# Reordering the attention steps, the range of the logits and the first gather of a fused HGRN2 and expert-routing kernel

## The chip, the cores and the metric

The kernel runs on one core of a Trainium2 chip, as one launch. The metric is the device time in microseconds (us). Before the change the median of three runs is 498.82 us (498.05 to 499.04); the profiled execution took 495.89 us, of which the trace spans 494.1 us. TensorE is called PE in profiles, its weight loads PEld; VectorE is DVE, ScalarE ACT, GpSimd POOL, SyncE SP.

## The reference

A gated linear attention (HGRN2) with 4 batches, 8 heads, 768 positions and a head size of 48 is followed by a layer of 8 experts with balanced assignment.

```python
def _attn_ref(q, k, v, f_logit):
    f = 1.0 / (1.0 + np.exp(-f_logit))
    state = np.zeros((B, H, D, D)); y = np.zeros_like(q)
    for t in range(S):
        state = f[:, :, t, :, None] * state + np.einsum('bhd,bhe->bhde', k[:, :, t], v[:, :, t])
        y[:, :, t] = np.einsum('bhd,bhde->bhe', q[:, :, t], state)
    return y

def _moe_ref(x, w_gate, w1, w2):          # x: 3072 tokens of 384
    logits = x @ w_gate                    # 3072 x 8
    # greedy: the largest logits first; each token gets one expert,
    # each expert takes at most cap = 3072 / 8 = 384 tokens
    for idx in np.argsort(-logits.flatten()): ...
    for e in range(E):
        out[assigned == e] = np.maximum(x[assigned == e] @ w1[e], 0.0) @ w2[e]
```

## The kernel before

The attention works on 24 chunks of 128 positions (6 for each of 4 batches). Each chunk runs through stages; a step holds one stage each of up to six chunks. The order of the parts is written down by hand, and each engine takes its instructions in this order. The number behind each part is its stage: how many steps ago its chunk began.

```python
    STEP = ((decayed, 2), (q_columns, 2), (k_columns, 2), (sums, 1), (transposed, 5),
            (factors, 1), (x_copy, 5), (k_copy, 2),
            (added, 2), (halves, 1), (gate, 5), (gated_q, 1), (new_state, 2), (decays, 0),
            (gated_k, 1), (span, 1), (to_logits, 5), (split, 0), (clamp, -1), (outputs, 4),
            (scores, 3))
    small = deque()

    def attention(first, last):
        for step in range(first, last):
            if step + AHEAD < len(chunks):
                load(chunks[step + AHEAD])
            for part, stage in STEP:
                if 0 <= step - stage < len(chunks):
                    part(chunks[step - stage])
                if part is split:
                    for _ in range(min(len(small), 4)):
                        small.popleft()()
```

`small` is a queue of little operations, constants for the routing at first, that are slipped into the steps. What the parts put on the engines:

- `q_columns`, `k_columns`: transposes T on TensorE; ScalarE copies qT, and `k_copy` on VectorE copies kT.
- `sums`: the products L of the decays with a triangle. `factors`: VectorE cuts them off (dl), ScalarE takes the exponentials eq and ek.
- `transposed`, `x_copy`, `gate`, `to_logits`: the finished rows x are transposed to X, VectorE copies xT, TensorE multiplies by the gate weights, VectorE copies the logits.
- `added`, `new_state`: the products dS of k and v for the carried state. `halves`: sums of the decays over half chunks, into the same bank as X. `span` copies these.
- `decays` (ScalarE), `split`: upper on VectorE, then high on ScalarE and low on GpSimd, the two terms for the next `sums`.
- `scores`: the products A of k and q, 32 small matmuls, and two masked copies am on VectorE.
- `outputs`: the values (am with v) and the state products (R with qT) in Y, and two copies of x on ScalarE:

```python
    def outputs(G):
        b, c = G["b"], G["c"]
        x = work.tile([128, D], FP32, name="x", tag="x", bufs=3)
        Y = [ps("Y", "sum") for _ in range(2)]
        for hp in range(HP):
            ...                      # Y <- am, v
        if G["R"] is not None:       # not in the first chunk of a batch
            ...                      # Y <- R, qT
        for par in range(2):
            nc.scalar.copy(out=..., in_=Y[par]...)
        row = S * b + C * c
        nc.scalar.dma_start(out=xd[row:row + C, :], in_=x[:])
        G["x"] = x
```

Near the end of the attention the range of the logits is found (`bounds`), for the thresholds of the search that follows. It takes two little matmuls:

```python
        def extremes():
            r = ps("bounds")
            ts(pair[:, 1:2], pair[:, 1:2], -1.0, ALU.mult)
            nc.tensor.transpose(out=r[0:2, 0:128], in_=pair[:], identity=ident[:])
            reduce(top[0:2, :], r[0:2, 0:128], ALU.max)
            ts(tops[0:2, :], ident[0:2, 0:2], top[0:2, :], ALU.mult)

        def spread():
            r = ps("bounds")
            nc.tensor.matmul(out=r[:, 0:2], lhsT=two[0:2, :], rhs=tops[0:2, :], start=True,
                             stop=True)
            nc.vector.tensor_copy(out=ends[:], in_=r[:, 0:2])
            reduce(width[:], ends[:], ALU.add)
        ...
        return [partial(lanes, 0, ALU.max), partial(lanes, 1, ALU.min), extremes, spread,
                one_step] + [partial(table, shift) for shift in SHIFTS]
```

Then come 8 rounds of routing, each with a search in five counting steps (`digit_alone` in the first round, `digit_beside` with expert matmuls between them later) and a list of the tokens of one expert: members, places, lines, comparisons in_line with the counts, and the token numbers. With these the rows xe are gathered from DRAM by an indirect DMA that GpSimd issues. `idle_turns(n, ...)` puts n matmuls of constants on TensorE; their result is not used.

```python
            def place():
                incl = rt([NT], "mincl")
                nc.vector.tensor_tensor_scan(incl[:], onesc[:], L["member"][:], 0.0,
                                             op0=ALU.mult, op1=ALU.add)
                total = rt([1], "total", BF16)
                nc.vector.tensor_copy(out=total[:], in_=incl[:, NT - 1:NT])
                r = bank("before", "r")
                nc.tensor.matmul(out=r[:, 0:1], lhsT=ltri[:], rhs=total[:], start=True, stop=True)
            ...
            def lines():
                stt(pl[:], L["incl"][:], L["r"][:, 0:1], L["member"][:], ALU.add, ALU.mult)
                tt(b[:], col(pl[:], TE - 1), row(beyond_block[:], TE - 1), ALU.is_ge)
                for i in range(TE - 2):
                    stt(pl[:], b[:, :, i], -128.0, pl[:], ALU.mult, ALU.add)
                stt(line[:], b[:, :, TE - 2], -128.0, pl[:], ALU.mult, ALU.add)
```

Of the kernel before, what the change touches and what calls it, by code (L numbers as in the profile page):

```python
# [11 lines left out]
FP32 = mybir.dt.float32  # L12
# [14 lines left out]
def kernel(  # L27
# [289 lines left out]
    def outputs(G):  # L317
        b, c = G["b"], G["c"]
        x = work.tile([128, D], FP32, name="x", tag="x", bufs=3)
        Y = [ps("Y", "sum") for _ in range(2)]  # L320
        for hp in range(HP):
            for par in range(2):
                for j in range(2):
# [4 lines left out]
                        start=(hp == 0), stop=False, skip_group_check=True)  # L328
        if G["R"] is not None:
# [9 lines left out]
        for par in range(2):  # L339
            nc.scalar.copy(  # L340
                out=x[:].rearrange("t (a r d) -> t r a d", r=2, d=DH)[:, par],
                in_=Y[par][:, 0:HP * DH].rearrange("t (a d) -> t a d", d=DH))
        row = S * b + C * c
        nc.scalar.dma_start(out=xd[row:row + C, :], in_=x[:])
        G["x"] = x
# [20 lines left out]
    def to_logits(G, to=None):  # L366
        if to is None:
# [11 lines left out]
    STEP = ((decayed, 2), (q_columns, 2), (k_columns, 2), (sums, 1), (transposed, 5),  # L379
            (factors, 1), (x_copy, 5), (k_copy, 2),  # L380
            (added, 2), (halves, 1), (gate, 5), (gated_q, 1), (new_state, 2), (decays, 0),
            (gated_k, 1), (span, 1), (to_logits, 5), (split, 0), (clamp, -1), (outputs, 4),
            (scores, 3))
    small = deque()

    def attention(first, last):
        for step in range(first, last):
            if step + AHEAD < len(chunks):
                load(chunks[step + AHEAD])
            for part, stage in STEP:  # L390
                if 0 <= step - stage < len(chunks):
                    part(chunks[step - stage])
                if part is split:
                    for _ in range(min(len(small), 4)):
                        small.popleft()()
# [38 lines left out]
    def ramp(n, name, step, base, when=later):  # L434
# [8 lines left out]
    later(nc.vector.tensor_copy, out=counts[:],  # L443
          in_=count_i[:].unsqueeze(2).to_broadcast((128, 128, 2)))
# [16 lines left out]
    beyond_block = ramp(TE - 1, "beyond_block", 128, 1)  # L461
# [66 lines left out]
    def bounds(c1):  # L528
# [6 lines left out]

        def lanes(at, op):
# [3 lines left out]

        def extremes():
            r = ps("bounds")
            ts(pair[:, 1:2], pair[:, 1:2], -1.0, ALU.mult)
            nc.tensor.transpose(out=r[0:2, 0:128], in_=pair[:], identity=ident[:])
            reduce(top[0:2, :], r[0:2, 0:128], ALU.max)
            ts(tops[0:2, :], ident[0:2, 0:2], top[0:2, :], ALU.mult)

        def spread():
            r = ps("bounds")
            nc.tensor.matmul(out=r[:, 0:2], lhsT=two[0:2, :], rhs=tops[0:2, :], start=True,  # L550
                             stop=True)
            nc.vector.tensor_copy(out=ends[:], in_=r[:, 0:2])
# [642 lines left out]
```

## Time and profile before

| stage | us from the start | what sets the pace |
|---|---|---|
| filling and regular steps | 0 to 119 | TensorE, with short waits |
| steps with the range of the logits | 119 to 152 | TensorE and VectorE in turn |
| drain of the attention | 152 to 173 | a chain through VectorE and TensorE |
| first routing and gather | 173 to 200 | VectorE, then the gather |
| experts and 7 more rounds | 200 to 494 | TensorE |

The page of the profile has these totals:

```text
PE 449.5 (91%) x4873; PEld 305.7 (62%) x4873; DVE 267.3 (54%) x890; ACT 137.6 (28%) x323; POOL 139.2 (28%) x195
DMA  8999998765001104417117027036045046701000
GB/s 169 194 207 208 200 203 191 171 148 127 35 19 41 44 2 165 140 28 274 50 57 262 34 82 255 16 122 213 17 140 195 17 149 215 294 11 38 0 27 27
```

Each digit or number is one fortieth of the span, 12.35 us. In lines of the timeline the columns are the start in us, the time until the last instruction of the group ends, the engine, the line of the kernel, the operation, output and inputs with their shapes, and the count. What stands in brackets is the idle time before the group, and which instruction ended it. Busy time of matmuls overlaps, as they are pipelined, so starts are better compared than durations.

### The profile page before, as it was taken

Reading aid. Unit: us, or ns where it says so; the run is one execution under the profiler, and the core shown is the slowest. Engines: PE = TensorE matmul, PEld = TensorE weight load, DVE = VectorE, ACT = ScalarE, POOL = GpSimd, SP = SyncE. Lnnn points to the kernel's source line nnn. Section 1 sums busy time; section 2 is a strip of 40 time slices with the busy share of each in tenths; the row PEclk is TensorE's granted clock in tenths of the full one; section 3 lists DMA queues with packets and bytes.
Section 4 is the critical chain, followed back from the end, with each engine's and each line's share of the span. In section 5 each row is a group of like instructions: output and inputs, shape, how many; then the busy total and the mean of one; then the engine's idle time right before and its main releaser. Section 6 shows DMA issues by size and latency. Waiting matters only on the chain.

```text
span 494.1 us, 11887 instructions
## 1 busy us (share of the span) xinstructions
PE 449.5 (91%) x4873; PEld 305.7 (62%) x4873; DVE 267.3 (54%) x890; ACT 137.6 (28%) x323; POOL 139.2 (28%) x195
## 2 busy tenths in 40 slices
PE   8989999997978648899999999999999998999992
PEld 4778888886877534446555556556555555556550
DVE  5788777677677373755655655654654655000000
ACT  3665655554343000110220210211211111112200
POOL 1566555555242003004105004014015005201010
PEclk9999999999789757999999999999999999999997
DMA  8999998765001104417117027036045046701000
GB/s 169 194 207 208 200 203 191 171 148 127 35 19 41 44 2 165 140 28 274 50 57 262 34 82 255 16 122 213 17 140 195 17 149 215 294 11 38 0 27 27
DMA packets 118400, 59.12 MB, mean 120 GB/s; under 512 B 101664, under 2 KB 112960, under 8 KB 118336
## 3 DMA queue, kind: packets, MB, share of 16 engines
q1 hardware_dynamic: 111760, 44.06, 34.0%
q0 software_dynamic: 3072, 9.44, 5.8%
q10 hardware_dynamic: 3504, 4.77, 2.7%
q8 instruction: 40, 0.66, 0.5%
q14 instruction: 24, 0.20, 0.1%
HBM read 48.77 MB, written 9.49 MB: 118 GB/s over the span
## 4 chain that ended last, share of the span: by engine, by line
PE 50%; issue 22%; DVE 16%; POOL 5%; ACT 3%; DMA 2%; POOLq 0%; DVEq 0%; ACTq 0%
PE O L973 15%; PE H L962 13%; PE A L307 4%; PE Y L324 4%; DVE am L312 4%; PE Y L334 3%; PE nothing L127 2%; DVE xT L356 2%; POOL xe L918 2%; POOL out_dram L978 2%; PE X L225 2%; PE T L254 2%; PE X L363 1%; DVE above L511 1%; PE cnt L712 1%
## 5 line engine op out<-in xcount | busy, mean ns | idle before, releaser
L962 PE MATMUL H<-xeT,w 128*128 128x384 f32 x384 | 136.0, 497 | 2.8 <-ACT xeT L954 2.4
L973 PE MATMUL O<-w,hT 128*128 128x384 f32 x384 | 129.3, 490 | 0.0
L973 PEld LDWEIGHTS O<-w,hT 128*128 128x128 f32 x384 | 71.3, 190 | 47.3 <-issue 2.0
L962 PEld LDWEIGHTS H<-xeT,w 128*128 128x128 f32 x384 | 68.4, 191 | 46.7 <-issue 8.4
L966 ACT ACTIVATE hT<-H 128x384 f32<-128x384 f32 x64 | 31.4, 490 | 112.5 <-PE H L962 103.3
L978 POOL DMA_INDIRECT out_dram<-o,token x24 | 24.7, 1029 | 111.0 <-ACT o L977 107.9
L312 DVE COPY_PREDICATED am<-mask,A 128x512 f32<-128x512 int32 x48 | 32.3, 725 | 29.2 <-PE A L307 29.2
L236 POOL TENSOR_TENSOR kg<-k,ek 128x384 f32<-128x384 f32 x23 | 29.7, 1291 | 60.1 <-ACT ek L214 60.1
L977 ACT COPY o<-O 128x384 f32<-128x384 f32 x24 | 11.5, 478 | 108.2 <-PE O L973 101.5
L875 POOL TENSOR_TENSOR past<-b,ramp_nt 128x48 f32<-128x48 f32 x8 | 2.4, 302 | 135.7 <-DVE b L504 135.7
L918 POOL DMA_INDIRECT xe<-xd,token x24 | 24.1, 1002 | 25.4 <-DVE used L508 15.0
L307 PE MATMUL A<-qT,kT 48*64 48x128 f32 x768 | 28.4, 284 | 0.1
L324 PE MATMUL Y<-v,am 128*64 128x48 f32 x768 | 27.3, 225 | 0.0
L324 PEld LDWEIGHTS Y<-v,am 128*64 128x64 f32 x768 | 24.8, 140 | 0.0
L127 PE MATMUL nothing<-idle,ones 128*128 128x384 bf16 x96 | 23.3, 398 | 1.5 <-DVE ones L132 1.5
L307 PEld LDWEIGHTS A<-qT,kT 48*64 48x64 f32 x768 | 22.7, 140 | 0.7 <-issue 0.5
L190 POOL TENSOR_TENSOR low<-g,upper 128x384 fp32r<-128x384 f32 x22 | 22.2, 1010 | 2.9 <-DVE upper L187 0.7
L954 ACT COPY xeT<-Xe 128x384 f32<-128x384 f32 x24 | 10.4, 488 | 41.5 <-PE Xe L951 37.4
L262 ACT COPY qT<-T 128x512 f32<-128x512 f32 x24 | 14.1, 586 | 20.3 <-PE T L254 19.8
L213 ACT ACTIVATE eq<-dl 128x384 f32<-128x384 f32 x24 | 12.5, 522 | 25.6 <-DVE dl L211 25.6
L225 PE MATMUL X<-ind,g 128*64 128x2 f32 x320 | 12.7, 200 | 7.7 <-DVE xT L356 7.7
L504 DVE TENSOR_TENSOR own<-cnt,mine 120x64 f32<-120x64 f32 x30 | 6.7, 224 | 20.4 <-PE cnt L712 18.5
(192 smaller groups left out, 639.7 us busy)
## 6 DMA issues: line engine op xcount, KB each, us to landing
w<-in_moe_w_dram SPq DMA_DIRECT2D x16, 1536.0 KB, 6.6
f<-in_f_logit_dram SPq DMA_DIRECT2D x24, 192.0 KB, 4.6
q<-in_q_dram SPq DMA_DIRECT2D x24, 192.0 KB, 4.4
k<-in_k_dram SPq DMA_DIRECT2D x24, 192.0 KB, 3.8
v<-in_v_dram SPq DMA_DIRECT2D x24, 192.0 KB, 4.3
xd<-x ACTq DMA_DIRECT2D x24, 192.0 KB, 3.1
xe<-xd,token POOLq DMA_INDIRECT x24
out_dram<-o,token POOLq DMA_INDIRECT x24
```

Source lines behind the costliest of these rows:

```text
L127: nc.tensor.matmul(out=nothing[:, 0:CAP], lhsT=ones[:], rhs=idle[:], start=True, stop=True)
L190: nc.gpsimd.tensor_tensor(out=low[:], in0=g[:, :, 0:DH], in1=upper[:].bitcast(FP32), op=ALU.subtract)
L225: nc.tensor.matmul(out=G["ends"][DP * r:DP * r + DP, :, hp], lhsT=g[:, 2 * hp + r, :], rhs=ind[:], start=True, stop=True)
L236: engine.tensor_tensor(out=G["kg"][:, :, 0:DH], in0=G["k"][:], in1=G["ek"][:], op=ALU.mult)
L307: nc.tensor.matmul(out=A[par][HC * j:HC * j + HC, 128 * hp:128 * hp + 128], lhsT=G["kT"][rows, hp, HC * j:HC * j + HC], rhs=G["qT"][rows, ...
L312: nc.vector.copy_predicated(am[:, par], mask[:].unsqueeze(1).to_broadcast((128, HP, 128)), A[par][:].rearrange("s (a t) -> s a t", t=128))
L324: nc.tensor.matmul(out=Y[par][HC * j:HC * j + HC, DH * hp:DH * hp + DH], lhsT=G["am"][:, par, hp, HC * j:HC * j + HC], rhs=G["v"][:, 2 * h ...
L918: nc.gpsimd.indirect_dma_start(out=xe[:], out_offset=None, in_=xd[:, :], in_offset=bass.IndirectOffsetOnAxis(ap=token[:, i:i + 1], axis=0))
L962: nc.tensor.matmul(out=L["H"][:, 0:CAP], lhsT=L["w1"][:, d, 128 * ft:128 * ft + 128], rhs=xT[:, d, :], start=(d == 0), stop=(d == DC - 1))
L966: nc.scalar.activation(out=hT[:, ft, :], in_=L["H"][:, 0:CAP], func=AF.Relu)
L973: nc.tensor.matmul(out=L["O"][:, 0:D], lhsT=hT[:, ft, 128 * i:128 * i + 128], rhs=L["w2"][:, ft, :], start=(ft == 0), stop=(ft == FC - 1))
L978: nc.gpsimd.indirect_dma_start(out=outs[next(tiles)][:, :], out_offset=bass.IndirectOffsetOnAxis(ap=L["token"][:, i:i + 1], axis=0), in_=o ...
```

## The change

It moves work to where its operands are ready and its wait is covered. There are six parts.

1. In each step the values are put between dS and the half sums, and X goes before L; VectorE copies xT ahead of dl.
2. The parts of `bounds` are spread over four steps; its two matmuls stand behind `sums` of the step after the one that made their operands. The queue `small` is served after the logits, before `split`.
3. The last steps have an order of their own, in which the gate comes last before A; for the last chunk one of the two copies of x goes to VectorE.
4. In the first list the xe buffers are touched by GpSimd early, so that what their memory was used for before is waited for there and not at the gather.
5. The list's chain is shorter: the flag of full experts is formed later, in `close`; the total is not copied; lines are counted by comparisons in units of 1/128, with b off the chain.
6. Idle matmuls: two behind the counts and two behind each digit of the first search; one in place of two between the pieces of the first list.

```diff
-    STEP = (...)                                  # as above
+    FIRST = ((decayed, 2), (q_columns, 2), (k_columns, 2), (transposed, 5), (sums, 1))
+    FILLING = (FIRST + ((x_copy, 5), (factors, 1), (k_copy, 2),
+                        (added, 2), (values, 4), (halves, 1), (gate, 5), (gated_q, 1),
+                        (new_state, 2), (decays, 0), (gated_k, 1), (span, 1), (to_logits, 5),
+                        (split, 0), (clamp, -1), (queries, 4), (scores, 3)))
+    LAST = FIRST + ((x_copy, 5), (k_copy, 2), (values, 4), (queries, 4), (gate, 5),
+                    (to_logits, 5), (scores, 3))
...
-            for part, stage in STEP:
+            for part, stage in FILLING if step < len(chunks) + 2 else LAST:
                 if 0 <= step - stage < len(chunks):
                     part(chunks[step - stage])
-                if part is split:
+                if part is sums and small_pe:
+                    small_pe.popleft()()
+                if part is to_logits:
                     for _ in range(min(len(small), 4)):
                         small.popleft()()
...                                                # outputs becomes values and queries; in queries:
-            nc.scalar.copy(
+            copy = nc.vector.tensor_copy if par and G["i"] == len(chunks) - 1 else nc.scalar.copy
...                                                # bounds
+        def turn():
+            rows["r"] = ps("bounds")
+            nc.tensor.transpose(out=rows["r"][0:2, 0:128], in_=pair[:], identity=ident[:])
+
         def extremes():
-            r = ps("bounds")
-            ts(pair[:, 1:2], pair[:, 1:2], -1.0, ALU.mult)
-            nc.tensor.transpose(out=r[0:2, 0:128], in_=pair[:], identity=ident[:])
-            reduce(top[0:2, :], r[0:2, 0:128], ALU.max)
+            reduce(top[0:2, :], rows["r"][0:2, 0:128], ALU.max)
...
+        return ([partial(lanes, 0, ALU.max), partial(lanes, 1, ALU.min), negated],
+                [turn, spread], [extremes], [widths, one_step],
+                [partial(table, shift) for shift in SHIFTS])
...                                                # digit_alone
+            idle_turns(2, bank("nothing", "O"))    # behind the counts
...
+            idle_turns(2, bank("nothing", "O"))    # behind the digit
...                                                # assign; close forms full instead
-            ts(full[:], places[:], 0.5, ALU.is_lt)
...                                                # members
+                if alone:
+                    L["xe"] = [rows() for _ in range(TE)]
+                    for xe in L["xe"]:
+                        nc.gpsimd.memset(xe[0:1, 0:1], 0.0)
-                tt(score[:], left[:], full[:], ALU.mult)
+                stt(score[:], places[:], 0.5, left[:], ALU.is_lt, ALU.mult)
...                                                # place
-                total = rt([1], "total", BF16)
-                nc.vector.tensor_copy(out=total[:], in_=incl[:, NT - 1:NT])
-                nc.tensor.matmul(out=r[:, 0:1], lhsT=ltri[:], rhs=total[:], start=True, stop=True)
+                nc.tensor.matmul(out=r[:, 0:1], lhsT=ltri[:], rhs=incl[:, NT - 1:NT], start=True,
+                                 stop=True)
+                member = rt([NT], "member_")
+                ts(member[:], taken[:], L["m"][:], ALU.is_equal, 1.0 / 128, ALU.mult)
...                                                # lines
+                at = rt([NT], "at")
+                stt(at[:], pl[:], 129.0 / 128, pl[:], ALU.is_ge, ALU.subtract)
+                for i in range(1, TE - 1):
+                    new = line if i == TE - 2 else rt([NT], "at")
+                    stt(new[:], pl[:], i + 129.0 / 128, at[:], ALU.is_ge, ALU.add)
+                    at = new
                 tt(b[:], col(pl[:], TE - 1), row(beyond_block[:], TE - 1), ALU.is_ge)
-                for i in range(TE - 2):
-                    stt(pl[:], b[:, :, i], -128.0, pl[:], ALU.mult, ALU.add)
-                stt(line[:], b[:, :, TE - 2], -128.0, pl[:], ALU.mult, ALU.add)
...                                                # between the pieces of the first list
-                        idle_turns(2, bank("nothing", "O"))
+                        idle_turns(1, bank("nothing", "O"))
...                                                # the end of the attention
-    small.extend(bounds(NCH - 2))
-    attention(ALL - 9, ALL - 5)
+    ends, small_of_pe, *more = bounds(NCH - 2)
+    small.extend(ends)
+    attention(ALL - 9, ALL - 8)
+    small_pe.extend(small_of_pe)
+    for step, pieces in enumerate(more, ALL - 8):
+        small.extend(pieces)
+        attention(step, step + 1)
```

## The prediction

> **What bounds the kernel now.** I read the stage windows first, to see which engine is full where; then the clock row; then the timeline of one regular step of the attention; then the places where TensorE stands still. In the windows the columns are each engine's busy time, the granted TensorE clock, the DMA share and GB/s.
>
> ```profile
> 97.00:119.00 22.00, 21.14 (x534) 18.84 (x525) 16.52 (x43) 12.40 (x32) 11.51 (x17) 1.00 0.77 169
> 119.00:152.00 33.00, 26.83 (x580) 23.96 (x577) 23.59 (x60) 14.05 (x36) 13.62 (x20) 0.84 0.08 28
> 152.00:173.00 21.00, 15.47 (x431) 13.33 (x428) 10.01 (x28) 2.95 (x10) 1.93 (x3) 0.87 0.11 41
> 173.00:184.00 11.00, 5.19 (x127) 4.38 (x128) 7.73 (x37) 0.00 (x0) 0.00 (x0) 0.50 0.01 1
> 236.00:273.00 37.00, 36.24 (x159) 21.55 (x158) 21.09 (x84) 6.60 (x14) 7.35 (x9) 1.00 0.35 122
> ```
> ```profile
> PEclk9999999999789757999999999999999999999997
> ```
>
> TensorE is nearly full in the attention up to 119 us and again from 200 us on, where the experts run (36.24 of 37.00 us). Between 119 and 200 us it is not full, and the clock falls in just those slices. The change touches the attention (0 to 173 us), the first routing (173 to 200 us) and a few small VectorE operations in each expert's list. From 200 us TensorE hides those, so I look for the gain before 200 us.
>
> A regular step takes 5.95 us (the first matmuls of am with v start at 107.37 and 113.31 us):
>
> ```profile
> 110.04 1.36 DVE L312 COPY_PREDICATED am<-mask,A 128x512 f32<-128x512 int32 x2 [1.41 <-PE A L307]
> 111.40 0.56 DVE L211 TENSOR_SCALAR dl<-L 128x384 f32<-128x384 f32 x1
> 111.87 0.55 DVE L356 COPY xT<-X 128x384 f32<-128x384 f32 x1
> 112.47 0.55 PEld L225 LDWEIGHTS X<-ind,g 128*64 128x64 f32 x16 [0.31 <-DVE xT L356]
> 113.31 1.12 PE L324 MATMUL Y<-v,am 128*64 128x48 f32 x32
> 114.36 0.68 PE L334 MATMUL Y<-R,qT 48*64 48x48 f32 x32
> 114.86 1.07 PE L307 MATMUL A<-qT,kT 48*64 48x128 f32 x32
> ```
>
> The half sums wait 0.31 us for xT, which VectorE copies only after the masks and dl. Elsewhere in the step TensorE goes from one group to the next. The range of the logits and the first gather look like this:
>
> ```profile
> 121.29 0.27 PE L544 MATMUL bounds<-ident,pair__2568 128*2 128x128 f32 x1 [1.82 <-ACT high L189]
> 122.26 0.38 PE L550 MATMUL bounds<-tops,two 2*128 2x2 f32 x2 [0.70 <-DVE tops L508]
> 124.79 1.95 PE L307 MATMUL A<-qT,kT 48*64 48x128 f32 x32
> 137.80 0.63 PE L225 MATMUL X<-ind,g 128*64 128x2 f32 x16 [2.07 <-DVE xT L356]
> ...
> 190.20 0.16 DVE L511 SCALAR_TENSOR_TENSOR token<-pair 128x3 int32<-128x3 f32 x1
> ...
> 192.98 1.21 POOL L918 DMA_INDIRECT xe<-xd,token  x1 [5.13 <-issue]
> ```
>
> The two range matmuls hold TensorE for 1.82 and 0.70 us, and after it the same 32 matmuls of A take 1.95 us instead of 1.07. The first gather starts 2.62 us after its token numbers are there.
>
> **What the Trainium skill says.** "TensorE: Matmul & The Clock Gate", section "What's actually happening", says that TensorE runs at half its clock after an idle window of about 3.4 us and needs about that long of work to get it back. The trace agrees on the half (1.95 against 1.07 us), but gaps of 1.82 and 0.70 us, close together, were already enough here. The same page, "Step-by-step: what each phase is for", says that matmuls stay in program order and only weight loads are pulled ahead: a range matmul that waits holds up all behind it, as at 121.29. "Perfetto Trace Analysis", section "Identifying Dependency Chains", says that an instruction with waits on several engines may get semaphore instructions put before it. The built program gives the first gather eleven semaphores to wait for and the gather of the next expert one; the next one starts 0.28 us after its tokens (266.37 to 266.65). "SBUF — State Buffer", section "SBUF: two separate sides", says that VectorE and GpSimd lock a shared port pair for a whole instruction. This fits the tables steps<-count, which take 0.22 us or 0.83 to 0.98 us for the same 15 elements, but nothing here shows the lock itself.
>
> **The change part by part.**
>
> Regular steps. TensorE's order was T, L, X, dS, half sums, gate, values, state products, A; it becomes T, X, L, dS, values, half sums, gate, state products, A, and VectorE copies xT before dl. I lay the old durations in the new order, with S the start of the masks: dS at S+1.58, values S+2.13, half sums S+3.17, gate S+3.64, state products S+3.98, A S+4.45, next T S+5.49. xT is ready at S+1.95, long before S+3.17. The step becomes 5.62 us, 0.33 less. There is a second loop to check: after the gate, the logits copy, upper (0.65), high, and only then ScalarE's two copies of x. With the old distances (upper to high 0.85, high to x 0.40, x 0.54) x is ready at S+6.2 and the next X wants it at S+6.32: it fits with about 0.1 to spare. Eleven steps between the values at 46.02 and 113.31 lose 0.33 each: 3.6 at most. I count 3.3, as that margin is thin.
>
> Filling steps. The small constants ran after upper and now run before it, and so before x. In the steps with no carried state (values at 29 to 46 us) there are no state products to cover it, and about 1.2 us of constants push x back by that much. I expect three steps of 5.5 to 5.7 us to become about 6.6, which costs 3.3; the wait for the count (1.39 us of VectorE at 25.92) mostly goes, as the iota comes before low: gain 1.3. Sum: a loss of 2.0.
>
> Range steps. The values at 113.31 and at 152.15 are 38.84 us apart over five steps, 9.1 more than five times 5.95. In the new order both range matmuls find their operands a step old. What stays is VectorE's work before upper, now 0.7 (lanes), 0.6 (extremes), 0.7 (width) and, with eight table operations of 0.15 to 0.2 in a single step, 1.4 us; less 0.1 of margin each that is about 3.0. Five steps of 5.62 and 3.0 make 31.1: a gain of 7.7.
>
> Drain. From the A of one step to that of the next it takes 4.86 us now: the masks, xT, gate 0.34, values 1.07, state products 0.47, A 1.04. In the new order the values wait for the masks alone, and xT with its wait (0.5) lies beside them: about 4.55. The next to last steps gain 0.45 and 0.28, and in the last the values start 0.6 earlier and x is copied by two engines at once (0.54 becomes about 0.3), perhaps with less time at half clock: 1.2. Sum: 1.9.
>
> First routing. Gone from the path are full<-places (0.20 from start to start) and the copy of the total (0.25); of the list's four operations the comparison b no longer waits for the one before it (0.05); one idle matmul instead of two between the pieces lets the tokens' matmuls start sooner (they start 0.4 us after their operands at 188.71 and 189.57): 0.3. Sum 0.8. The four idle matmuls put into each of five counting rounds cost 0.2 us a round as long as they run at half clock (two take 0.64 us, the gap is 0.43), and then give a full clock to what follows: I set both against each other as 0.
>
> First gather. Touching the xe buffers early meets the waits while GpSimd is idle: 2.62 becomes 0.28 us, a gain of 2.34. The 27 idle matmuls behind the tokens take about 4.4 us at full clock, and the first rows would land after about 4.0, but what the experts wait for is the third block, 2.57 us later, so they hide.
>
> Experts. Each list loses about 0.5 us of VectorE, but TensorE is the bound there; its only waits for VectorE from 200 us on are 2.4 + 1.1 + 1.0 us: I count 0.
>
> Sum: 3.3 - 2.0 + 7.7 + 1.9 + 0.8 + 0.0 + 2.3 = 14.0 us off 498.8.
>
> **Rivals.** First, x takes the place of xT: TensorE then waits at X for ScalarE's copy in every step, and the regular and range steps give back what they won. For it: the new margin is 0.1 us, and the constants and range work now lie ahead of upper. Against it: the old distances just fit. If the wait were 0.3 us a step over twenty steps, 6 us would be gone and the time would be about 491. Second, DMA becomes the bound: its share is 0.91 to 0.97 up to 97 us. Against it: a step moves 960 KB (four loads, one store), which at the 200 to 208 GB/s of the full slices takes about 4.7 us, less than 5.62; and the load queue mostly waits for buffers. If it did bind, the 3.3 of the regular steps would fall away: 488. Third, the clock: if the new waits in the range steps and the idle matmuls in the counting still leave the half clock, about 3 us come back: 488. In the other direction, if the small work does not push x at all, the filling loss and most of the 3.0 vanish: 480.
>
> **Range and chances.** 498.8 - 14.0 gives 484.8; I write 485.0. The largest term, 7.7 for the range, rests on gaps that are seen in the trace and on operands that are a step old; 2.3 for the gather rests on a like case in the same trace. Those two alone make 10.0 us, which is the 2% line (488.8). The rest is small and of both signs. The range is 480.5 to 490.5. Faster by over 2%: 0.82; within 2%: 0.16; slower: 0.02.
>
> **What would show it.** The half sums should have no wait for xT, and the step should be 5.6 to 5.7 us. The range matmuls should show no wait, and the clock row should have no fall at 120 to 145 us. X in the filling steps should wait over 1 us for x. The first gather should start about 0.3 us after its token. From the first expert matmul to the end the time should be as before. I would be wrong if X waits for x in every step, if the half clock stays at 120 to 145 us, or if the experts' stage gets longer.

## The result, and the profile after

The changed kernel takes 478.2 us (median of four runs, 477.48 to 484.76) where the kernel before takes 498.93 beside it: a ratio of 0.958, with a 95% interval of 0.956 to 0.961. The prediction was 485.0, with a range of 480.5 to 490.5: the direction was right, the gain larger than the range allowed. On a second chip the same two kernels took 498.04 and 480.63 us; there the result lies just inside the range. The traced executions last 494.1 and 475.5 us, so 18.6 us of the difference can be followed in them.

Milestones that both traces have cut the 18.6 us into stretches. A step is counted so that the A of the first chunk falls in step 3; "A 19" is the start of the first matmul of A in step 19; "last logits" is the end of VectorE's last copy of logits in the attention.

| stretch | before, us | after, us | gain | predicted |
|---|---|---|---|---|
| start to A 3 | 17.80 | 16.66 | 1.14 | 0 |
| A 3 to A 8 (filling) | 29.77 | 28.35 | 1.42 | -2.0 |
| A 8 to A 19 (regular) | 67.29 | 63.48 | 3.81 | 3.3 |
| A 19 to A 24 (range) | 38.84 | 28.50 | 10.34 | 7.7 |
| A 24 to the last logits (drain) | 18.72 | 15.99 | 2.73 | 1.9 |
| last logits to first expert matmul | 27.62 | 28.54 | -0.92 | 3.1 |
| from there to the end | 294.06 | 293.95 | 0.11 | 0.0 |

The first line is not the change's doing. TensorE starts both kernels with the same 19 idle matmuls; they take 6.07 us in the one trace and 4.83 in the other, and in a second trace of the unaltered changed kernel 6.01, with A 3 at 17.73. That leaves 17.5 us for the change, 3.5 more than the 14.0 predicted. Three terms are well off, and not all to one side: the filling steps by +3.4, the range by +2.6, the first routing with its gather by -4.0.

The stage windows of the kernel after (columns: window and its length; busy time of PE, PEld, DVE, ACT and POOL; clock, DMA share, GB/s), and its clock row:

```profile
91.00:108.50 17.50, 17.50 (x511) 16.15 (x509) 13.74 (x35) 11.31 (x29) 10.83 (x17) 1.00 1.00 209
108.50:137.00 28.50, 27.11 (x734) 24.45 (x728) 24.18 (x72) 17.11 (x43) 14.87 (x24) 1.00 0.21 59
137.00:153.00 16.00, 13.36 (x368) 11.16 (x360) 9.89 (x24) 2.62 (x9) 1.30 (x3) 1.00 0.15 52
153.00:164.00 11.00, 9.89 (x137) 4.66 (x138) 6.61 (x32) 0.00 (x0) 0.16 (x3) 0.59 0.01 2
218.00:255.00 37.00, 36.23 (x164) 21.81 (x163) 20.59 (x83) 7.16 (x16) 8.42 (x9) 1.00 0.33 118
```
```profile
PEclk9999999999999569999999999999999999999997
```

TensorE is full for the whole of 91 to 108.5 us, with no wait left (17.50 of 17.50), and DMA is full beside it. In the range steps the clock is whole. One dip is left, which begins in the counting: TensorE is busy there for 9.89 of 11.00 us (before, 5.19 of 11.00), yet the clock is 0.59. That busy time is idle matmuls, and it buys nothing.

The timeline of the kernel after: a regular step, then the two range matmuls and the one long wait of the range steps, then the first list.

```profile
99.37 0.49 PE L351 MATMUL X<-ident,x 128*128 128x128 f32 x3
100.14 0.67 PE L284 MATMUL dS<-v,kg 128*64 128x48 f32 x16
100.64 1.10 PE L322 MATMUL Y<-v,am 128*64 128x48 f32 x32
101.58 0.60 PE L225 MATMUL X<-ind,g 128*64 128x2 f32 x16
...
116.62 0.27 PE L553 MATMUL bounds<-ident,pair__2567 128*2 128x128 f32 x1
123.19 0.38 PE L561 MATMUL bounds<-tops,two 2*128 2x2 f32 x2
133.81 0.55 PE L351 MATMUL X<-ident,x 128*128 128x128 f32 x3 [0.79 <-ACT x L343]
...
171.35 0.36 PE L936 MATMUL tokens<-number,in_line 128*128 128x6 bf16 x8 [2.54 <-POOL number L912]
172.64 6.03 PE L127 MATMUL nothing<-idle,ones 128*128 128x384 bf16 x28
178.50 0.49 PE L983 MATMUL Xe<-ident,xe 128*128 128x128 f32 x3
...
169.43 1.36 POOL L910 TENSOR_SCALAR past<-b,lane 128x48 f32<-128x48 f32 x1
173.47 1.21 POOL L951 DMA_INDIRECT xe<-xd,token  x1 [2.17 <-DVE token L519]
```

Of the kernel before, GpSimd's lane operation; and of the kernel after, two windows over the 28 idle matmuls (columns as above):

```profile
186.73 0.41 POOL L877 TENSOR_SCALAR past<-b,lane 128x48 f32<-128x48 f32 x1
```
```profile
172.64:175.40 2.76, 2.76 (x15) 1.31 (x12) 0.33 (x2) 0.00 (x0) 1.62 (x2) 0.51 0.78 319
175.40:178.60 3.20, 3.20 (x21) 2.00 (x20) 1.11 (x8) 0.00 (x0) 1.65 (x4) 1.00 0.60 164
```

The half sums (X from ind and g) no longer carry a wait, and neither range matmul does. What is new stands in the last five lines of the timeline: the tokens wait 2.54 us for GpSimd's number, GpSimd's lane operation takes 1.36 us where it took 0.41 before, and the 28 idle matmuls then run for 6.03 us, the first 2.76 us of them at half clock, until 5.03 us after the first gather began.

### The profile page after: what moved, and what is told of

It reads as the page before. It is cut to its first block, busy times and chain, and to the rows that moved or that the text cites. A ratio compares the mean times of both kernels' runs of the same rounds, so it can differ in the third digit from the quotient of the medians.

```text
span 475.5 us, 11928 instructions
## 1 busy us (share of the span) xinstructions
PE 444.0 (93%) x4886; PEld 298.7 (63%) x4886; DVE 258.9 (54%) x890; ACT 138.1 (29%) x322; POOL 139.8 (29%) x198
## 4 chain that ended last, share of the span: by engine, by line
PE 36%; issue 19%; DVE 7%; POOL 4%; DMA 1%; ACT 1%; POOLq 0%; ACTq 0%
PE O L1005 15%; PE H L994 13%; PE nothing L127 3%; POOL out_dram L1010 2%; POOL xe L951 1%; PE cnt L731 1%; PE tokens L936 1%; DVE above L519 1%; DVE fillsb L512 1%; DVE filledb L522 1%; PE cnt L712 1%; DMA xe<-xd,token 1%; DVE count L522 1%; DVE sized L754 1%; PE cnt L746 0%
## 5 line engine op out<-in xcount | busy, mean ns | idle before, releaser
L908 POOL TENSOR_TENSOR past<-b,ramp_nt 128x48 f32<-128x48 f32 x8 | 4.5, 563 | 120.0 <-DVE b L512 120.0
L236 POOL TENSOR_TENSOR kg<-k,ek 128x384 f32<-128x384 f32 x23 | 23.1, 1006 | 46.6 <-ACT ek L214 46.6
L127 PE MATMUL nothing<-idle,ones 128*128 128x384 bf16 x109 | 28.7, 404 | 1.5 <-DVE ones L132 1.5
L307 PE MATMUL A<-qT,kT 48*64 48x128 f32 x768 | 26.9, 273 | 1.3 <-issue 0.9
L307 PEld LDWEIGHTS A<-qT,kT 48*64 48x64 f32 x768 | 21.3, 133 | 2.0 <-issue 1.4
L516 DVE TENSOR_SCALAR pair<-tokens 128x6 f32<-128x6 f32 x8 | 1.3, 165 | 31.8 <-PE tokens L936 31.8
L731 PEld LDWEIGHTS <-above 128*120 128x120 bf16 x90 | 9.0, 133 | 13.4 <-DVE above L519 9.1
```

The source lines that it names most:

```text
L127: nc.tensor.matmul(out=nothing[:, 0:CAP], lhsT=ones[:], rhs=idle[:], start=True, stop=True)
L236: engine.tensor_tensor(out=G["kg"][:, :, 0:DH], in0=G["k"][:], in1=G["ek"][:], op=ALU.mult)
L307: nc.tensor.matmul(out=A[par][HC * j:HC * j + HC, 128 * hp:128 * hp + 128], lhsT=G["kT"][rows, hp, HC * j:HC * j + HC], rhs=G["qT"][rows, ...
```

## The experiments

On the chips that ran the variants, single times of one kernel spread by up to 2.3 per cent (the kernel before took 495.02 to 506.54 us), and the traces have stops of 0.2 to 1.9 us in the attention that no releaser in the profile explains. So I compare stretches. Seven traces have the same attention: two of the changed kernel (the second, on another chip, is `after_again`) and five of variants that alter only the first routing.

| stretch | first trace of after | after_again | all seven |
|---|---|---|---|
| A 3 to A 8 | 28.35 | 28.32 | 28.32 to 28.36 |
| A 8 to A 19 | 63.48 | 68.26 | 63.48 to 68.26, median 65.39 |
| A 19 to A 24 | 28.50 | 28.44 | 28.44 to 30.91 |
| last logits to first expert matmul | 28.54 | 28.58 | (the routing differs) |

The first and last repeat well; the two in the middle hold the stops, and the half clock that follows some of them. The longest stop is in after_again, before A, and behind it the clock is at half (0.50 from 65.1 to 68.5 us):

```profile
64.87 1.81 PE L307 MATMUL A<-qT,kT 48*64 48x128 f32 x32 [1.94 <-ACT x L343]
```

### The first routing: three edits, alone and together

`count_without_idle`:

```
                                 start=(c == 0), stop=(c == NT - 1))
-            idle_turns(2, bank("nothing", "O"))
...
                             stop=True)
-            idle_turns(2, bank("nothing", "O"))
             return digit, ALU.add
```

> The changed kernel without the four idle matmuls of each of the five counting rounds. Theory 1 (they only cost: two of them take 0.82 us at half clock where the gap is shorter, and the clock does not come back): a round goes from 2.31 back to 1.90 us, and the time falls by 2.0 us, from 478.2 to about 476.2. Theory 2 (my prediction: what they cost is paid back by the clock of what follows): the list and the first expert matmuls get slower, and the time stays at 478.2 within 0.5.

Measured: from the last logits to the first expert matmul 26.77 us instead of 28.54, 1.77 less. The median time, 479.77, has no changed kernel beside it on the same chip and spreads from 477.62 to 481.59; the ratio to before is 0.961 (0.956 to 0.966). The timeline of a counting round, first of the kernel after, then of this variant:

```profile
159.55 0.82 PE L127 MATMUL nothing<-idle,ones 128*128 128x384 bf16 x2
159.84 0.15 DVE L522 TENSOR_REDUCE filled<-fills 15x1 bf16<-15x8 f32 x1
160.30 0.18 PE L720 MATMUL cnt<-filled,unit 15*128 15x1 bf16 x1
160.51 0.87 DVE L519 SCALAR_TENSOR_TENSOR above<-over,cnt,steps 128x120 bf16<-128x120 f32 x3 [0.38 <-PE cnt L720]
```
```profile
160.93 0.15 DVE L522 TENSOR_REDUCE filled<-fills 15x1 bf16<-15x8 f32 x1
161.13 0.16 PE L719 MATMUL cnt<-filled,unit 15*128 15x1 bf16 x1 [0.43 <-DVE filled L522]
161.33 0.86 DVE L519 SCALAR_TENSOR_TENSOR above<-over,cnt,steps 128x120 bf16<-128x120 f32 x3
```

From filled to the next above it is 0.67 us with the idle matmuls and 0.40 without: the digit's matmul stands in line behind 0.82 us of idle work, though its operand, filled, is done at 159.99. The clock row of the variant is the same as that of the kernel after, digit for digit. So the matmuls cost 1.8 us and bought no clock; theory 1 holds.

`b_ahead`:

```
                 stt(pl[:], L["incl"][:], L["r"][:, 0:1], L["member"][:], ALU.add, ALU.mult)
+                tt(b[:], col(pl[:], TE - 1), row(beyond_block[:], TE - 1), ALU.is_ge)
                 at = rt([NT], "at")
...
-                tt(b[:], col(pl[:], TE - 1), row(beyond_block[:], TE - 1), ALU.is_ge)
```

> The changed kernel with the comparison b moved from just before in_line to just after pl, so that GpSimd's three operations on it start two VectorE operations earlier. Theory 1 (GpSimd's operations run against VectorE's in_line and are the last operand of the first tokens matmul): GpSimd's lane operation falls from 1.36 towards 0.4 us, the wait of 2.54 us for number becomes under 1.5, and the time falls by 1.0 to 1.5, to about 477.0. Theory 2 (the tokens wait for the last piece of in_line anyway): the wait moves to in_line and the time stays at 478.2 within 0.4.

Measured: from the last logits to the first tokens matmul 16.86 us instead of 18.37, so 1.51 sooner. The timeline of the variant:

```profile
173.71 0.42 POOL L910 TENSOR_SCALAR past<-b,lane 128x48 f32<-128x48 f32 x1
174.88 0.35 PE L936 MATMUL tokens<-number,in_line 128*128 128x6 bf16 x8 [1.09 <-POOL number L912]
176.27 6.80 PE L127 MATMUL nothing<-idle,ones 128*128 128x384 bf16 x28
182.91 0.49 PE L983 MATMUL Xe<-ident,xe 128*128 128x128 f32 x3
```

Lane is back at 0.42 us and the wait at 1.09. Theory 1 holds for the tokens, but only 0.63 us of it reaches the experts: the idle matmuls, which the gather does not need, now take 6.80 us. How much gets through varies with the moment at which the clock comes back: in seven other traces with the same code behind the tokens, it is 10.12 to 11.04 us from the first tokens matmul to the first expert matmul, and 11.04 in b_ahead. The median time, 479.97 (478.52 to 482.34), does not show it.

`idle_14`:

```
-                    idle_turns(27, bank("nothing", "O"))
+                    idle_turns(14, bank("nothing", "O"))
```

> The changed kernel with 14 idle matmuls instead of 27 behind the tokens of the first list. Theory 1 (they hold up the first transpose of the gathered rows by some 1.5 us): the first transpose starts when the first block has landed, about 1.2 to 1.5 us sooner, and the time falls by about 1.0, to 477.2. Theory 2 (my prediction: the third block is what the first expert matmul waits for): the first expert matmul starts at the same distance from the last token matmul and the time stays at 478.2 within 0.3. Theory 3: the clock falls without them, and the time is 479 or more.

Measured: 0.92 us less from the last logits to the first expert matmul; the gain in time (481.57 us, 478.03 to 482.11) is lost in the spread. The timeline of the variant:

```profile
178.40 1.21 POOL L951 DMA_INDIRECT xe<-xd,token  x1 [2.17 <-DVE token L519]
181.71 0.55 PE L983 MATMUL Xe<-ident,xe 128*128 128x128 f32 x3 [0.26 <-DMA xe<-xd,token]
184.39 0.55 PE L983 MATMUL Xe<-ident,xe 128*128 128x128 f32 x3 [0.20 <-DMA xe<-xd,token]
185.51 0.91 PE L994 MATMUL H<-xeT,w 128*128 128x384 f32 x2 [0.57 <-ACT xeT L986]
```

The first transpose now comes 3.31 us after the gather (5.03 after the change), and the first and third blocks wait for their data, as they should. The experts start 7.11 us after the gather, as in the kernel before (7.06), instead of 8.05. Theory 1 holds; theory 2 would have needed the third block to be the limit with 27 idle matmuls as well, and it was not.

`three_mended` joins the three edits.

> The three edits together: no idle matmuls in the counting, b just after pl, 14 idle matmuls behind the tokens. Theory 1, if the three costs lie one behind the other: 2.0 + 1.2 + 1.0 = 4.2 us off 478.2, about 474.0, and from the last logits to the first expert matmul about 24.5 us instead of 28.7. Theory 2, if the idle matmuls hold the clock for one another: less than 2 us off, 476.5 or more.

Measured: 24.79 us from the last logits to the first expert matmul, 3.75 less than the changed kernel: more than the three alone add up to (3.33), as the tokens' gain now gets through. Its time was 477.7 us (476.77 to 479.31), with no changed kernel beside it, so it ran again next to the unaltered changed kernel (`after_again`):

> The changed kernel unaltered, beside its variants on the same chip. All theories: the stretches between the milestones of the trace repeat within 0.3 us where TensorE has no stop that the profile leaves unexplained; from the last logits to the first expert matmul 28.7 us.

> The three edits to the first routing once more, beside the unaltered changed kernel. If the 3.7 us that the trace of the first run shows between the last logits and the first expert matmul are real: the time is 3.2 to 4.0 us below that of the changed kernel on the same chip. If they were a hazard of one profile: under 1.5 us.

Measured: 475.46 us (475.05 to 477.91) against 480.63 (478.41 to 483.12) for the changed kernel on the same chip; the ratios to before are 0.955 (0.951 to 0.960) and 0.965 (0.961 to 0.970), and do not overlap. The stretch is 24.37 against 28.58 us, a gain of 4.2; the rest of the 5.2 us between the medians lies within the spread of the attention. This version beats both kernels.

### The filling steps and the range

`small_late` undoes the new place of the small work in the changed kernel; `before_small_early` makes that one edit in the kernel before:

```
-                if part is to_logits:          # small_late; the reverse in before_small_early
+                if part is split:
                     for _ in range(min(len(small), 4)):
                         small.popleft()()
```

> The changed kernel with the small work (constants, range pieces) put back behind upper, as before the change. Theory 1 (ahead of upper the small work fills the time in which kg holds GpSimd, and upper then runs alone in 0.36 instead of 0.65 us, so that x is not pushed back): nothing is won by putting it back; 478.2 to 480. Theory 2 (my prediction's filling step: the small work ahead of upper pushes x back by about 1.1 us in three steps): X waits less for x in the filling steps, and the time falls by about 2 to 3 us, to 475.7.

> The kernel before with one edit: the small work is served ahead of upper instead of behind it. Theory 1 (less running of VectorE against GpSimd's kg in those steps): the stretch up to the ninth A is about 1.5 us shorter, and the time falls by 1 to 2, to about 497.3. Theory 2 (my prediction): x is pushed back in the filling steps, and the time rises by about 2, to 500.9. Theory 3: the gain of the filling steps comes from the order of the matmuls, and this edit alone makes no difference within 0.6.

`range_together` undoes the division of the range work in the changed kernel: extremes begins with negated() and turn(), widths with spread(), and all of it goes through one list again. `before_range_behind` brings only the divided range work into the kernel before.

> The changed kernel with each range matmul back in one piece with the operations that make its operands and read its result. Theory 1 (the range matmuls a step behind are worth what I had counted, and what I missed came from the base step): 7 to 8 us are lost in the range steps, about 486. Theory 2 (the pieces are worth the whole 10.3 us of the range steps): about 488.5. Theory 3 (values early and the other order already shorten the waits): under 5 lost, below 483.

> The kernel before with one edit: the range matmuls a step behind their operands, in the same five steps, everything else in its old order. Theory 1 (the pieces act by themselves): the range steps gain 7 to 8 us, 498.9 becomes about 491, and the half clock at 120 to 145 us is gone. Theory 2 (the order of values and half sums is needed too, as the halves wait for xT which the range pieces push back): under 5 us gained, 494 or more, and the waits for xT grow in those steps.

Measured, in the two stretches, with the parts of the change that each kernel has (S: small work ahead of upper; P: range matmuls a step behind; O: the new order of the step):

| kernel | parts | A 3 to A 8 | A 19 to A 24 | median time (range), us |
|---|---|---|---|---|
| before | none | 29.77 | 38.84 | 498.93 (498.05 to 499.33) |
| before_small_early | S | 28.87 | 35.69 | 492.47 (490.1 to 495.06) |
| before_range_behind | P | 29.75 | 32.54 | 492.09 (488.4 to 499.2) |
| range_together | S, O | 28.33 | 31.39 | 483.74 (482.13 to 485.14) |
| small_late | P, O | 29.35 | 29.95 | 482.86 (480.99 to 483.9) |
| after | S, P, O | 28.35 | 28.50 | 478.2 (477.48 to 484.76) |

The times of the four variants come from one chip, where the kernel before took 497.62 (496.36 to 506.05). Two executions over 1.5% above the fastest of their kernel, 499.2 in before_range_behind and 484.76 in after, belong to a slower state of the chip; without them these medians are 490.55 and 477.59. Stops without a releaser of 0.72 us in small_late and 0.60 in after are contained in the range column. Each figure is from one trace: in the filling column the seven traces above differ by 0.04 us, in the range column by 2.5, so that there a smaller difference counts only with a wait that explains it.

Filling. The small work ahead of upper gains 0.90 us in the old order and 1.00 in the new one, the new order 0.40 and 0.54; together they make the 1.42. My prediction had expected a loss of 2.0 here. For small_late theory 1 holds, though its time, 482.86, lies above the 480 I had allowed: 1.00 us is lost in the filling and 1.45 in the range, the latter within the spread. For before_small_early it holds too, with 0.90 in place of about 1.5 us; the time fell further than I said, as the range gains more than the filling.

Two things make up the gain. In the old order 0.66 of the 0.90 us fall between A 4 and A 5 (6.84 us, with S 6.18): VectorE waits there for GpSimd's count, 1.39 us before and 0.80 with S, and only before do the masks behind that wait hold up dS, by 0.39 us. In the new order this step gives 0.09 us and the three after it 0.91. There, and in the rest of the old order, the cause shows in the timelines, first of the kernel before:

```profile
25.92 0.23 DVE L395 CAST count<-count_i 128x128 f32<-128x128 int32 x1 [1.39 <-POOL count_i L395]
28.95 1.35 POOL L236 TENSOR_TENSOR kg<-k,ek 128x384 f32<-128x384 f32 x1 [2.44 <-ACT ek L214]
29.87 0.65 DVE L187 TENSOR_SCALAR upper<-g 128x384 int32<-128x384 int32 x1
36.18 1.01 POOL L190 TENSOR_TENSOR low<-g,upper 128x384 fp32r<-128x384 f32 x1
36.23 1.00 DVE L395 TENSOR_SCALAR ramp_nt<-count 128x24 f32<-128x24 f32 x1
```

Then of before_small_early:

```profile
24.02 0.23 DVE L395 CAST count<-count_i 128x128 f32<-128x128 int32 x1 [0.80 <-POOL count_i L395]
33.44 1.35 POOL L236 TENSOR_TENSOR kg<-k,ek 128x384 f32<-128x384 f32 x1 [0.45 <-ACT ek L214]
34.52 0.31 DVE L395 TENSOR_SCALAR ramp_nt<-count 128x24 f32<-128x24 f32 x1
35.02 0.29 DVE L187 TENSOR_SCALAR upper<-g 128x384 int32<-128x384 int32 x1
```

And of small_late:

```profile
35.83 0.36 DVE L187 TENSOR_SCALAR upper<-g 128x384 int32<-128x384 int32 x1 [0.41 <-ACT g L177]
36.37 1.00 DVE L402 TENSOR_SCALAR ramp_nt<-count 128x24 f32<-128x24 f32 x1
37.37 0.55 PE L351 MATMUL X<-ident,x 128*128 128x128 f32 x3 [0.43 <-ACT x L343]
```

Add start and duration: in the kernel before, upper ends at 30.52 and kg at 30.30; ramp_nt, 24 elements, ends at 37.23 and low at 37.19. Both VectorE operations end with GpSimd's, whatever their own size. Behind upper, small work meets low, which starts as soon as upper is there, and waits it out; ahead of upper it has free time, since upper cannot end before kg does (kernel before) or start before ScalarE's g is there (0.41 us idle in small_late). Then ramp_nt takes 0.31 and upper 0.29 us, and x is hardly pushed back: in the filling steps X waits 0.50, 0.43 and 0.50 us in small_late (the last for VectorE's past, not for x), and 0.47, 0.34 and 0.22 in the kernel after. "SBUF — State Buffer", section "SBUF: two separate sides", says that the loser of the port pair shared by the two engines is blocked for the other's whole instruction; these common ends are what that looks like, and the prediction, which named it, said that nothing showed it.

Range. Into the kernel before, S alone brings 3.15 us and P alone 6.30; put last, S brings 1.45 and P 2.89. O brings 4.30 on top of S and 2.59 on top of P. The gains overlap, as all act on the same waits; those of 1.45 to 2.89 us lie within the spread or near it. The timelines of before_range_behind and of range_together show what each lacks:

```profile
130.10 0.63 PE L225 MATMUL X<-ind,g 128*64 128x2 f32 x16 [0.65 <-DVE xT L356]
136.04 0.63 PE L225 MATMUL X<-ind,g 128*64 128x2 f32 x16 [0.79 <-DVE xT L356]
142.64 0.63 PE L225 MATMUL X<-ind,g 128*64 128x2 f32 x16 [1.44 <-DVE xT L356]
```
```profile
118.28 0.27 PE L553 MATMUL bounds<-ident,pair__2567 128*2 128x128 f32 x1 [1.13 <-DVE pair__2567 L516]
119.17 0.38 PE L563 MATMUL bounds<-tops,two 2*128 2x2 f32 x2 [0.62 <-DVE tops L516]
129.72 0.55 PE L351 MATMUL X<-ident,x 128*128 128x128 f32 x3 [0.52 <-ACT x L343]
```

With P alone, the range matmuls wait for nothing, but the half sums still wait for xT, up to 1.44 us. They wait even in the last three of these steps, where there are no dS matmuls (the last chunk of a batch leaves no state, and dS ends at 130.6 us in the kernel before): TensorE has half a microsecond less to do there, and the old order turns it into waiting. In the new order it becomes time: one step without dS takes 5.08 us (125.85 to 130.93) against 5.52 with it. With S and O alone, the range matmuls wait 1.13 and 0.62 us, less than the 1.82 and 0.70 of before, and the clock is at half from 119.8 us on for 3.4 us, where it was for 6.8 before.

For the numbers I had set: range_together loses 2.9 us, theory 3 (under 5 us; the time of 483.74 is just above the 483 I gave it). before_range_behind gains 6.3 in the stretch, between its two theories: the half clock is gone from 120 to 143.5 us, as theory 1 says, but it comes once more for 3.4 us at 143.6, after the wait of 1.44 us; and the waits for xT grow, as theory 2 says.

### The regular step

`gate_ahead` and `xT_late` each undo one part of the new order:

```
-                        (added, 2), (values, 4), (halves, 1), (gate, 5), (gated_q, 1),
+                        (added, 2), (halves, 1), (gate, 5), (values, 4), (gated_q, 1),   # gate_ahead
...
-    FILLING = (FIRST + ((x_copy, 5), (factors, 1), (k_copy, 2),
+    FILLING = (FIRST + ((factors, 1), (x_copy, 5), (k_copy, 2),                          # xT_late
```

> The changed kernel with the half sums and the gate ahead of the values again; xT stays ahead of dl, and X ahead of L. Theory 1 (the place of the values is what keeps VectorE's upper off GpSimd's kg: the late gate holds the copies of span and logits, so upper starts when kg has ended): upper takes 0.6 us again in the regular steps, x comes later, and X waits for it 0.1 to 0.3 us a step; the regular step goes from 5.52 to 5.6 or 5.7 us and the time rises by 2 to 3. Theory 2 (TensorE sets the regular step alone, and only the wait for xT had to go): 5.5 us a step and the same time within 0.6.

> The changed kernel with VectorE's copy of xT behind dl again; the values stay ahead of the half sums. Theory 1 (xT first moves ek and kg half a us later against qg, which is why kg takes 1.00 instead of 1.35 us): kg takes 1.35 again, but the half sums do not wait for xT, as the values cover it, so that the regular step stays at 5.5 us; the time is the same within 0.6. Theory 2 (xT first is what takes the wait away): the half sums wait for xT again by 0.2 us or more a step, the time rises by 3 or more.

Measured: 480.81 us (479.17 to 482.73) and 481.18 (480.33 to 482.53), against 480.63 for the changed kernel on the same chip. An unbroken regular step takes 5.56 and 5.52 us (5.52 after, 5.95 before). Of kg, the tile's own view has this line (minimum, median and maximum in ns, first and last start) in gate_ahead and in xT_late:

```profile
L236 POOL TENSOR_TENSOR kg<-k,ek x23: 1000/1005/1016, 14.0 to 140.6; 128x384 f32<-128x384 f32 x23
```
```profile
L236 POOL TENSOR_TENSOR kg<-k,ek x23: 1000/1340/1352, 12.9 to 138.1; 128x384 f32<-128x384 f32 x23
```

My first theory of gate_ahead fell: upper stays at 0.36 us with the gate ahead, and the step grows by 0.04 us. For xT_late theory 1 holds: kg is back at 1.34 us, the half sums do not wait, and nothing is lost in the regular step. So it is xT ahead of dl that frees kg (ek, and with it kg, comes half a microsecond later, when VectorE's qg is nearly done), while for the regular step either edit is enough: both remove the wait for xT, and then TensorE's own work sets 5.5 us. Both variants keep X ahead of L, which brings xT forward too; whether that alone would do was not tried. The two do not repeat each other everywhere: A 3 to A 8 takes 28.84 us in xT_late, 0.49 more, and in the range steps of gate_ahead the half sums wait 0.30 us for xT again. A 19 to A 24 takes 29.14 us in gate_ahead and 29.37 in xT_late, which lies within the spread.

## Why the prediction was too cautious

**Filling steps, -2.0: the step that failed.** I took "x pushed back by about 1.2 us" as if VectorE's work ahead of upper were added to a full queue. The trace of before had the evidence against it: upper waits for g or for kg's end, and the small work behind it waits out low. The stretch gained 1.42 us where a loss of 2.0 was forecast, and the small work's place 0.9 to 1.0 of it. X waits for x 0.47 us at most, where I had expected over 1. A lesser slip went the other way: the wait for the count is 0.71 us after, against 1.39, so it halved and did not mostly go. That the small work might not push x at all, for a time of 480 us, stood among the rivals; it came close to what happened and had no weight in the sum.

**Range steps, 7.7: mechanism right, two terms mis-sized.** Both range matmuls are free of waits, and nothing in the change lowers the clock there (in two of the seven traces a stop of 1.13 or 1.23 us at A 20 does). The leftover of 3.0 for VectorE's work ahead of upper measured 0.79 at one X, in the step with the tables; the lanes, extremes and width hide. The base of five times 5.62, 28.1 us, comes to 27.1 (28.50 less that wait and a stop of 0.60): it overlooked that three of the five steps have no dS, of which the one without wait or range matmul takes 5.08 us.

**First routing, +0.8 with the idle matmuls set to 0: the other step that failed.** I had balanced a cost against a clock that would come back; count_without_idle shows 1.8 us of cost and no clock. Nor had I seen that b, moved to the end of its chain, starts GpSimd's three operations just when VectorE begins in_line, which reads two operands: 1.5 us at the tokens. The saved operations (places tested directly, no copy of the total) could not make up for that.

**First gather, 2.34: right.** From the token to the gather it is 0.30 us instead of 2.62, and the profile has one semaphore wait at the gather instead of nine (eleven in the built program, by the prediction). Undoing the touch alone was not tried. But "so they hide" for the 27 idle matmuls was wrong: I reckoned 4.4 us at full clock, and with the one before them they take 6.03, as the clock comes back only 2.8 us after their start; 0.9 us is lost there (idle_14).

**Regular steps 3.3: mechanism right, the size partly luck.** The wait for xT is gone, and the unbroken step is 5.52 us rather than 5.62, which over eleven steps would give 4.7. But the 3.81 of the first trace is the best of seven: their median of 65.39 us makes it 1.9 against the 67.29 of before, and after_again, with 68.26, shows no gain at all. What the order wins, the stops largely take back, for a cause that stays open.

**Drain 1.9, experts 0: right**, with 2.73 and 0.11. In the drain A 24 to A 26 gains 0.59 (0.73 said), and the last step 2.14 (1.2 said): it now runs at full clock throughout, which I had only held possible.

**The rivals.** X takes the place of xT as the place that waits, but only where small work precedes it, and for 0.2 to 0.8 us. DMA does not bind the unbroken step, though its share is 1.00 at 91 to 108.5 us; whether it has a part in the stops, no run tested. The errors partly cancelled: without the loss in the first routing the time would have been lower still, near what three_mended shows.

Open: the stops in the attention that no releaser explains (0.71 us at 86.82 and 0.60 at 120.22 in the kernel after, up to 1.94 in after_again). Their sizes change from trace to trace, their places hardly: step 11 and step 15 run long in all fourteen traces, in the kernel before too (6.43 and 6.92 us against 5.95), and step 10 in all eleven of the new order. No experiment here settles what they are.

## What to carry to other kernels

Before an operation moved ahead of another is charged to the path, ask what the other was waiting for: work put into a wait is free, and work taken from behind a shared-port rival even gains. Idle matmuls are not free either: they stand in TensorE's order ahead of whatever comes next, so give them a place only where the next operand is surely later than their end, reckoned at the clock that the trace grants there, and drop them where the clock row does not answer. And when two waits lie at one spot, removing one shows only part of its worth; measure the parts alone and left out before adding them up. Last, trace the same kernel twice before a stretch is credited to the change: here one repeated within 0.04 us and its neighbour only within 4.8.

## What the hardware showed beyond expectation

- A VectorE tensor-scalar operation or copy on SBUF that meets a GpSimd operation on SBUF can last until that one ends: 24 elements (ramp_nt) took 1.00 us beside low, 0.31 in the last part of kg (before_small_early), and 0.17 just after kg (34.19 us in the kernel after). Not all do: a single column (pair, at 120.99 us in the kernel before) took 0.15 us in the middle of low. In kg the reverse holds: 1.34 to 1.35 us when it starts together with qg, and 1.00 to 1.01 in the kernel after, where it starts when qg is nearly done.
- A short stop of TensorE can cost more than itself. In idle_14 it stands still for 0.75 us before A (87.71 us), and the clock is at half from 88.0 to 91.4 us; in the kernel after a stop of 0.71 us at the same place (86.82 us) leaves it whole.
- The 19 idle matmuls at the start took 4.83 or 6.01 us in two traces of the very same kernel, which moves all that follows by 1.1 us. "TensorE: Matmul & The Clock Gate", section "What's actually happening", says of the clock's warming up that it varies from run to run, as its window runs free of the kernel; the traces agree.
- Idle matmuls of 0.82 us, two sets in each counting round of 2.31 us, did not bring the clock back in 11 us: 9.89 us of it count as busy, and the granted clock is 0.59. The sets are broken by the counting's small matmuls and waits; no run here shows which share of busy time would have been enough.
